# The setup of a fused attention and state-space kernel: zero products on TensorE before x lands, fewer transfers in another order, and six scores ahead of the other chunks' last projections

## The chip, the cores and the metric

The kernel runs on one core of a Trainium2 chip. The metric is the device time of one execution in microseconds (us). Before the change three runs gave 1181.41, 1182.49 and 1183.07: a median of 1182.49.

## The reference

Two independent parts are computed and joined along the last axis. Part A is a diagonal state-space layer: for each of 576 channels a kernel of 2048 taps is summed from 128 complex exponentials, and u is convolved with it. Part B is attention with 32 query heads of width 18 and one shared key and value head, over 2048 positions.

```python
K = jnp.einsum("dn,dnl,dn->dl", Cc, jnp.exp(logdA[:, :, None] * l), dB).real   # part A
a = causal_convolution(u, K) + u * Dskip
q = (x @ wq).reshape(B, S, 32, 18)                                             # part B
k, v = x @ wk, x @ wv
p = softmax(q k^T * 18 ** -0.5);  b = (p v).reshape(B, S, 576) @ wo
return jnp.concatenate([a, b], axis=-1)
```

## The kernel before

**The tiling.** The 2048 positions are four chunks of 512 columns. Part B goes over 1024 score tiles: chunk c of the queries, group g of four heads, block kb of 128 keys, pair j of two heads. A score (`scores`, L492) is two fp16 matmuls of 55 rows: the augmented queries of a pair (`aug`, a ring of five tiles) against the augmented keys (`kaug`). High and low fp16 parts of q and k and one row of offsets stand on those 55 rows, which is why a projection is rounded into a high part (h1, h2) and a low part (l1, l2) and copied by DMA to rows 0, 18 and 36. ScalarE takes the exponential of each score (`exponentials`, L503), into one of ten P tiles. TensorE multiplies P by v (`product`, L793). NS = 3 scores make a round, as three PSUM tiles hold them.

Part A (class `Conv`, L958 on) runs beside it, mostly on VectorE: `arguments` (L1017) and `factors` (L1065) build exponentials, sines and cosines for a slice of 48 channels, `tables`, `kgen` and `back` the rest.

**The setup** (`Attention.setup`, L231) starts both parts. Loads go out on the queues of SP, ScalarE and POOL. `first` (p1) is the projection of x's chunk 0: the first 96 query columns and the keys, in five steps over the model dimension, x0 being loaded in five slices. `rest(k)` (L297) is step k of five for the keys of chunks 1 to 3 (`second`, p2), the last 32 of the first 128 query columns and all values (`vps`); it reads slice k of xr, x's chunks 1 to 3. From `first` come h1 and l1, whose copies fill chunk 0 of `kaug` (`place`, L340) and `aug` 0 and 1 (L318). `km`, `small`, `aw_first` and `bias` bound the scores so that the exponentials cannot overflow. `conv.begin(n)` (L1347) advances part A's first slice by n pieces, which puts these into the order of VectorE and ScalarE at that place. After `rest(4)` come h2 and l2, chunk 1 of `kaug`, and `vt`.

**The order of the work.** The order on TensorE, ScalarE and VectorE is the program's own order; POOL and SP are ordered by the framework. `main` (L740) goes round by round: scores, exponentials, then `fill` puts pieces of the query projections, of the output projection and of part A where a planner's clock (`Clock`, K.t for TensorE, K.v for VectorE, K.a for ScalarE) expects TensorE to wait. After the first round (three scores, r == 0) it calls `settle` (L346), which transposes v, makes `kmax` on TensorE (`kmx`), places chunks 2 and 3 of `kaug`, loads wq 2 to 4 and the rest of part A's inputs, and moves the planner's clock on by 2.0.

Of the kernel before, what the change touches and what calls it, by code (L numbers as in the profile page):

```python
# [17 lines left out]
P = 128  # L18
# [22 lines left out]
FLOOR = LIMIT / (2 * SCALE) * QQ / 60000.0  # L41

NS = 3
NP = 10


# [147 lines left out]
class Attention:  # L194
# [33 lines left out]
    def load_wq(self, m):  # L228
        self.nc.sync.dma_start(self.wq[m], self.a["wq"][m, :, :, :MQ[m][1]])

    def setup(self, tp, conv):  # L231

# [12 lines left out]
        wkv = tp.tile([P, 5, 64], F32, name="wkv_sb")  # L245
        xr = tp.tile([P, 5, 3, CT], F32, name="xr")
# [6 lines left out]
        vt = keys[:, 4, :]  # L253
        self.x0 = x0 = self.xp.tile([P, 5, CT], F32, name="x0", tag="x")

        nc.gpsimd.memset(x0[64:, 4, :], 0.0)
        nc.gpsimd.memset(xr[64:, 4], 0.0)
        for j in range(2):
            nc.gpsimd.memset(self.ring[j], 0.0)
        conv.early()  # L260
        nc.scalar.dma_start(self.wq[0], a["wq"][0])
        nc.sync.dma_start(wkv, a["wkv"])
        for k in range(5):
            n = DT[k][1]
            nc.sync.dma_start(x0[:n, k, :], a["xT"][0, :n, k, :])
        nc.scalar.dma_start(self.sel, a["sel"][:, 0:45])
# [14 lines left out]
        self.o_left = self.q_left = self.units = 0  # L281
        self.todo, self.busy, self.group = [], False, 0
        self.side_work = Stream(self.side(), self.k, 99.0)
        conv.begin(6)
        p1, small = (self.ps_s.tile([P, 2, CT], F32, tag="s", name=n)[:, 0, :] for n in ("first", "small"))
        p2 = self.bank(CT, "second")
        pv = self.ps_o.tile([P, CT], F32, tag="o", name="vps")
# [3 lines left out]
                             start=(k == 0), stop=(k == 4), tile_position=(0, 32 * j))  # L291

        def project(ps, j, i, c, k):
            nc.tensor.matmul(ps[32 * j:32 * j + 32, :], wkv[:, k, i:i + 32], xr[:, k, c - 1, :] if c else x0[:, k, :],
                             start=(k == 0), stop=(k == 4), tile_position=(0, 32 * j))

        def rest(k):  # L297
# [8 lines left out]
            project(p1, 3, 0, 0, k)  # L306
        nc.scalar.activation(h1, p1, AF.Copy, scale=QS)
        self.ab0 = ab = self.p2.tile([P, 2], F32, tag="ab", name="ab0_0")
        V.tensor_reduce(ab[:, 0:1], p1, axis=AX.X, op=ALU.max, apply_absolute_value=True)
        V.scalar_tensor_tensor(l1, p1, QS, h1, op0=ALU.mult, op1=ALU.subtract)  # L310
        V.tensor_scalar(ab[:, 0:1], ab[:, 0:1], QS, None, op0=ALU.mult)
        self.place(0, h1, l1, 96, (nc.sync, nc.sync))
        for pr in range(2):
            for row, src in ((0, h1), (18, h1), (36, l1)):
                for j in range(2):
                    h, b = 2 * pr + j, 64 * j + row
                    q = nc.sync if pr and row == 36 else nc.gpsimd
                    q.dma_start(self.aug[pr][b:b + 18, :], src[h * DH:h * DH + DH, :])  # L318
        V.tensor_scalar(self.km[:, 0:1], ab[:, 0:1], spread[:, 139:140], None, op0=ALU.mult)
# [13 lines left out]
        V.scalar_tensor_tensor(l2, p2, QS, h2, op0=ALU.mult, op1=ALU.subtract)  # L333
        self.place(1, h2, l2, 0, (nc.sync, nc.gpsimd))
        V.tensor_copy(vt, pv)
        V.tensor_reduce(self.km[:, 4:5], p2, axis=AX.X, op=ALU.max, apply_absolute_value=True)
        V.tensor_scalar(self.km[:, 4:5], self.km[:, 4:5], QS, None, op0=ALU.mult)
        self.vt = vt

    def place(self, c, hi, lo, i, qs):  # L340
        for row, t in ((0, hi), (36, hi), (18, lo)):
            for j in range(2):
                b = 64 * j + row
                qs[j].dma_start(self.kaug[b:b + 18, c * CT:(c + 1) * CT], t[i:i + 18, :])

    def settle(self, conv):  # L346

        nc, V, K = self.nc, self.V, self.k
        km, ab, spread = self.km, self.ab0, self.spread
        h2, l2 = self.parts[2:]  # L350
        vp = self.bank(CT, "vp").rearrange("p (j n) -> p j n", j=4)
        for j in range(4):
            nc.tensor.transpose(vp[:, j, :], self.vt[:, j * P:(j + 1) * P], self.ident)
        for src, dst in ((ab[96:, 0:1], ab[96:, 1:2]), (km[96:, 4:5], ab[96:, 0:1]), (ab[96:, 1:2], km[96:, 4:5])):
            V.tensor_copy(dst, src)
        V.tensor_scalar(km[:, 0:4], spread[:, 136:140], km[:, 4:5], None, op0=ALU.mult)
        V.tensor_copy(self.v[:, :, :DH].rearrange("p (c j) d -> p c j d", j=4), vp.rearrange("p j (c d) -> p c j d", c=4)[:, :, :, :DH])
        pk = self.bank(20, "kmx")
        for m in range(5):
            for b, n in ((0, 128),) if m < 4 else ((0, 64), (64, 64)):  # L360
                nc.tensor.matmul(pk[b:b + n, 4 * m:4 * m + 4], spread[:, 2 * m:2 * m + n], km[:, 0:4], start=True, stop=True, tile_position=(0, b))
# [378 lines left out]
    def main(self, conv, flag):  # L740
# [71 lines left out]
        for r in range(0, len(pairs), NS):  # L812
# [145 lines left out]
class Conv:  # L958
# [34 lines left out]
    def load(self, k):  # L993

        if k >= NCK:
            return
        nc = self.nc
        raw = self.p0.tile([P, 6, ND], F32, tag="raw", name=f"raw{k}")
        dt = self.p0.tile([P, ND], F32, tag="dt", name=f"dt{k}")
        nc.sync.dma_start(dt, self.a["ldt"][k * ND:(k + 1) * ND].partition_broadcast(P))  # L1000
        nc.sync.dma_start(raw, self.a["prm"][k])
        self.raw[k] = raw, dt

    def load_u(self, k):
        if k >= NCK:
            return
        nc = self.nc
        ut = self.p0.tile([P, 4, NE], F32, tag="u", name=f"u{k}")
        if k < 2:
            nc.vector.memset(ut[0:1, 0, 0:1], 0.0)  # L1010
        dsk = self.p0.tile([P, NE], F32, tag="dsk", name=f"dsk{k}")
        nc.sync.dma_start(ut, self.a["u"][k])
        nc.sync.dma_start(dsk, self.a["dsk"][k].partition_broadcast(P))
        self.ut[k] = ut, dsk
        self.ut_ready[k % 2] = self.k.t + 10.0

    def arguments(self, k, f, r, m):  # L1017
# [11 lines left out]
        tt(w[:, 0, :], cr, br, op=mu)  # L1029
        tt(w[:, 2, :], ci, bi, op=mu)  # L1030
        tt(w[:, 0, :], w[:, 0, :], w[:, 2, :], op=sb)
        tt(w[:, 1, :], cr, bi, op=mu)
        tt(w[:, 2, :], ci, br, op=mu)
        tt(w[:, 1, :], w[:, 1, :], w[:, 2, :], op=ad)
# [16 lines left out]
        yield "v", 0.0, False  # L1051
        if k == 0:
            tt(m, ch(av, NF), row(1), op=mu)
            yield "v", 0.0, False

    def restore(self, k):
# [342 lines left out]
def build(tc, **aps):  # L1399
# [3 lines left out]
    with ExitStack() as ctx:  # L1403
        clock = Clock()
        at = Attention(tc, ctx, aps, clock)
        cv = Conv(tc, ctx, at.bank, aps, clock)
        cv.at, at.conv = at, cv
        with tc.manual_schedule(engines={mybir.EngineType.PE, mybir.EngineType.Activation, mybir.EngineType.DVE}):
            with tc.tile_pool(name="setup", bufs=1) as tp:
                cv.setup()  # L1410
                at.setup(tp, cv)
            cv.open(ctx)
            at.open(ctx)
            at.main(cv, flag)
    ok = nc.values_load(flag[0:1, 0:1], min_val=0, max_val=1)
    with tc.If(ok < 1):
# [78 lines left out]
```

## Time and profile before

| What | Value |
|---|---|
| median of three runs | 1182.49 us |
| the profiled execution | 1183.13 us, span 1181.4 us |
| TensorE matmul, ScalarE, VectorE, POOL busy | 1090.5, 1032.4, 977.6, 129.6 us |
| mean granted TensorE clock | 0.988 |
| exponentials (L510 and L508) | 992 of 1033 ns, 32 of 1118 ns |
| first matmul, first score, first exponential | 7.86, 26.96, 27.80 us |

The rows in the prediction come from the page and from these views: the timeline of an engine (start, length, engine, line, operation, tiles, count, and in brackets the idle time before and what ended it; neighbours of one kind are merged), the chain of waits in order of time, tables by stretch (length, then busy time of PE, PEld, DVE, ACT and POOL with counts, the granted clock, the DMA share, GB/s), the groups of one tile, and the list of who waited for whom (us in total, times, longest).

### The profile page before, as it was taken

To read this page: it belongs to the slowest core of one execution; us is meant where nothing else is said; L and a number is where in the kernel's file an instruction comes from. 1 tells how busy PE (TensorE), PEld (TensorE's weight loads), DVE (VectorE), ACT (ScalarE), POOL (GpSimd) and SP (SyncE) were. 2 spreads that over 40 slices of the span, in tenths; PEclk is the share of its full clock that TensorE was granted. 3 is DMA by queue.
4 is the path that set the end of the run, shared out by engine and by line. 5 is a ranking of instruction groups with operands and counts; after the bars stand their busy time and mean duration, and the time that the engine had idled before them with its cause. 6 is when DMAs were issued, how large, how long until landed. Compare 5 with 4: busy or idle time off the path is not lost.

```text
span 1181.4 us, 32882 instructions
## 1 busy us (share of the span) xinstructions
PE 1090.5 (92%) x13862; PEld 393.2 (33%) x13862; DVE 977.6 (83%) x1576; ACT 1032.4 (87%) x1090; POOL 129.6 (11%) x233
## 2 busy tenths in 40 slices
PE   6999799999899999899999899999899999989997
PEld 1333233333333333333333333333333333323232
DVE  4678987988988996988998988988978995895923
ACT  3888998888989888998989899898999988898994
POOL 4330301110310100010120200000320000000000
PEclk9899899999999999999999999999999999999999
DMA  7412323122233102033213122012223112011111
GB/s 221 137 52 66 115 88 112 32 57 79 75 124 110 33 28 92 31 104 111 74 50 119 35 86 88 29 57 82 73 67 120 41 38 76 24 56 65 33 42 43
DMA packets 58398, 87.50 MB, mean 74 GB/s; under 512 B 15779, under 2 KB 34839, under 8 KB 57733
## 3 DMA queue, kind: packets, MB, share of 16 engines
q1 hardware_dynamic: 46821, 77.52, 20.5%
q0 software_dynamic: 10848, 7.37, 2.5%
q8 instruction: 110, 1.80, 0.7%
q10 hardware_dynamic: 576, 0.45, 0.1%
q14 instruction: 43, 0.35, 0.1%
HBM read 48.67 MB, written 35.91 MB: 72 GB/s over the span
## 4 chain that ended last, share of the span: by engine, by line
PE 52%; DVE 28%; ACT 10%; issue 6%; DMA 2%; SPq 0%; DVEq 0%; ACTq 0%
PE ops L800 21%; PE s L499 14%; ACT P L510 9%; DVE tab L117 5%; DVE acc L117 5%; PE op L191 4%; DVE ks L117 3%; DVE pt L117 3%; PE iy L191 3%; PE kg L1180 3%; PE q L393 2%; DMA wq_sb<-wq 2%; DVE tt L117 1%; PE hu L191 1%; PE lu L191 1%
## 5 line engine op out<-in xcount | busy, mean ns | idle before, releaser
L510 ACT ACTIVATE P<-s 128x1024 f32<-128x1024 f32 x992 | 935.3, 1033 | 107.0 <-PE s L499 105.4
L800 PE MATMUL ops<-P,v_sb 128*32 128x512 f32 x4096 | 513.5, 599 | 9.6 <-DVE o L121 9.4
L499 PE MATMUL s<-aug,kaug 55*128 55x512 f16 x2048 | 310.0, 383 | 50.1 <-ACT P L510 46.1
L499 PEld LDWEIGHTS <-kaug 55*128 55x128 f16 x2048 | 91.8, 94 | 385.6 <-issue 345.1
L800 PEld LDWEIGHTS ops<-P,v_sb 128*32 128x32 f32 x4096 | 116.8, 110 | 165.2 <-issue 123.8
L443 POOL DMA_DIRECT2D qd<-qh x116 | 66.5, 580 | 475.5 <-DVE qh L125 473.0
L191 PE MATMUL op<-wo_sb,oT 126*32 126x288 f32 (+1 forms) x1152 | 84.0, 416 | 5.5 <-DVE ob L121 2.5
L393 PE MATMUL q<-x,wq_sb 128*32 128x256 f32 x1360 | 85.3, 388 | 1.3 <-DVE un L133 1.3
L117 DVE TENSOR_TENSOR tab<-tab,tt 128x576 f32<-128x576 f32 (+1 forms) x72 | 59.1, 821 | 1.7
L117 DVE TENSOR_TENSOR tab<-r,dif 128x576 f32<-128x576 f32 (+1 forms) x72 | 58.9, 818 | 0.0
L117 DVE TENSOR_TENSOR tt<-f,sum 128x576 f32<-128x576 f32 (+1 forms) x72 | 58.9, 817 | 0.0
L117 DVE TENSOR_TENSOR tab<-sum,r 128x576 f32<-128x576 f32 (+1 forms) x72 | 58.8, 817 | 0.0
L117 DVE TENSOR_TENSOR tab<-tab 128x576 f32<-128x576 f32 (+1 forms) x72 | 58.8, 817 | 0.0
L393 PEld LDWEIGHTS q<-x,wq_sb 128*32 128x32 f32 x1360 | 40.3, 111 | 41.7 <-issue 16.5
L121 DVE COPY ksb<-kg 128x192 f32<-128x192 f32 x48 | 17.5, 364 | 42.9 <-PE kg L1180 42.8
L191 PEld LDWEIGHTS op<-wo_sb,oT 126*32 126x32 f32 (+1 forms) x1152 | 32.7, 111 | 50.0 <-issue 17.1
L117 DVE TENSOR_TENSOR acc<-acc,pt 128x1728 f32<-128x1728 f32 (+2 forms) x36 | 48.6, 1351 | 0.3
L117 DVE TENSOR_TENSOR pt<-us,ks 128x1728 f32<-128x1728 f32 (+2 forms) x36 | 48.3, 1350 | 0.1
L508 ACT ACTIVATE P<-s,bias 128x1024 f32<-128x1024 f32 x32 | 33.1, 1118 | 13.8 <-PE s L499 13.5
L1180 PEld LDWEIGHTS kg<-tab 128*32 128x32 f32 x2304 | 36.2, 110 | 25.8 <-issue 9.5
L1180 PE MATMUL kg<-tab 128*32 128x64 f32 x2304 | 41.7, 220 | 1.9 <-DVE tab L117 1.1
L117 DVE TENSOR_TENSOR ks<-ks 128x576 f32<-128x576 f32 (+1 forms) x48 | 41.0, 854 | 0.6
(155 smaller groups left out, 998.2 us busy)
## 6 DMA issues: line engine op xcount, KB each, us to landing
od<-o SPq DMA_DIRECT2D x31, 256.0 KB
aug<-qd SPq DMA_DIRECT2D x124, 55.0 KB
fr<-stage SPq DMA_DIRECT2D x10, 624.0 KB
u<-u SPq DMA_DIRECT2D x12, 384.0 KB
kd<-ksb SPq DMA_DIRECT2D x12, 384.0 KB
kt<-kd SPq DMA_DIRECT2D x48, 96.0 KB
outa<-u SPq DMA_DIRECT2D x12, 384.0 KB
oT<-od SPq DMA_DIRECT2D x16, 252.0 KB
```

The lines of the kernel that those rows point to most:

```text
L117: return self.v.tensor_tensor(out, *a, **k)
L121: return self.v.tensor_copy(out, *a, **k)
L191: nc.tensor.matmul(ps[j:e], w[:, j:e], x, start=start, stop=stop, tile_position=(0, j))
L393: nc.tensor.matmul(ps[o, 256 * f:256 * f + 256], w[:, k, i], xt[:, k, x], start=(k == 0), stop=(k == 4), tile_position=(0, 32 * j))
L443: q.dma_start(qd[h:h + n, row + d:row + d + nd, cs], src[i1:i1 + n * nd, :cs.stop - cs.start])
L499: nc.tensor.matmul(ps[:, j, :], self.kaug[r, kb * P:(kb + 1) * P], t[r, :], start=True, stop=True)
L508: nc.scalar.activation(pt, ps, AF.Exp, bias=self.bias, scale=SCALE / QQ)
L510: nc.scalar.activation(pt, ps, AF.Exp, scale=SCALE / QQ)
L800: nc.tensor.matmul(o_ps[32 * j:32 * j + 32, :], self.v[:, kb, :], pts[2 * n + j // 2][:, j % 2, :], start=(kb == 0), stop=(kb == 15), tile ...
L1180: nc.tensor.matmul(ps[32 * g:32 * g + 32, d, :], t[:, :32], t[:, 32:], start=(j == 0), stop=(j == 1), tile_position=(0, 32 * g))
```

## The change

Loads. x0 comes in three transfers (slices 0, 1 and 2, 3 and 4) in place of five, all of 128 partitions, so the memsets of the padding go. wq 0 is issued first. sel and spread move from ScalarE's queue to POOL's. xr becomes five tiles, each loaded by one transfer with 6 KB contiguous a partition, on POOL's queue behind a small copy that waits for x0's first slice; they take memory that part A uses later. wq 1 goes out after the copies.

TensorE. Three `matmul4` of zeros (WARM = 3) stand ahead of `first`.

Copies. `aug` 0 and 1 are filled by SP alone, chunk 0 of `kaug` by ScalarE, each set split so that h1's rows go before l1's.

Order. The pieces of part A are begun 4, 2 and 4 instead of 6 and 4, its first slice's coefficients are computed later, and later loads are held by small memsets. `rest(3)` stands behind the first three scores, `rest(4)` and what follows from it (`last`) behind the next three, and `settle` between the eighth and the ninth score. The planner's clock is set to 3.4, 5.3 and at least 8.8 there. POOL's order becomes the program's too.

```diff
+WARM = 3
-        nc.gpsimd.memset(x0[64:, 4, :], 0.0)
-        nc.gpsimd.memset(xr[64:, 4], 0.0)
+        nc.scalar.dma_start(self.wq[0], a["wq"][0])
         conv.early()
-        nc.scalar.dma_start(self.wq[0], a["wq"][0])
+        V.memset(self.wo[:, 0, :], 0.0)
+        warm = self.bank(CT, "warm")
+        for _ in range(WARM):
+            matmul4(nc, warm, self.wo[:, 0, 0:P], self.wo[:, 0, 0:CT])
         nc.sync.dma_start(wkv, a["wkv"])
-        for k in range(5):
-            n = DT[k][1]
-            nc.sync.dma_start(x0[:n, k, :], a["xT"][0, :n, k, :])
-        nc.scalar.dma_start(self.sel, a["sel"][:, 0:45])
-        nc.scalar.dma_start(spread[:, 0:140], a["sel"][:, 45:185])
-        for k in range(5):
-            n = DT[k][1]
-            nc.sync.dma_start(xr[:n, k], a["xT"][1:4, :n, k, :].rearrange("c p n -> p c n"))
+        for k0, k1 in ((0, 1), (1, 3), (3, 5)):
+            nc.sync.dma_start(x0[:, k0:k1, :], a["xT"][0, :, k0:k1, :])
         for b in (54, 118):
             nc.gpsimd.dma_start(self.kaug[b:b + 1, :], a["ones"])
+        nc.gpsimd.dma_start(self.sel, a["sel"][:, 0:45])
+        nc.gpsimd.dma_start(spread[:, 0:140], a["sel"][:, 45:185])
         nc.gpsimd.dma_start(self.ident, a["ident"])
-        self.load_wq(1)
+        nc.gpsimd.tensor_copy(xr[0][0:1, 0, 0:1], x0[0:1, 0, 0:1])
+        for k in range(5):
+            nc.gpsimd.dma_start(xr[k], a["xg"][k * P:(k + 1) * P, CT:].rearrange("p (c n) -> p c n", n=CT))
...
-        conv.begin(6)
+        conv.begin(4)
...
-        self.place(0, h1, l1, 96, (nc.sync, nc.sync))
-        for pr in range(2):
-            for row, src in ((0, h1), (18, h1), (36, l1)):
+        def first(pr, rows, q):
+            for row, src in rows:
                 for j in range(2):
                     h, b = 2 * pr + j, 64 * j + row
-                    q = nc.sync if pr and row == 36 else nc.gpsimd
                     q.dma_start(self.aug[pr][b:b + 18, :], src[h * DH:h * DH + DH, :])
+        self.place(0, h1, l1, 96, (nc.scalar, nc.scalar), (0, 36))
+        first(0, ((0, h1), (18, h1)), nc.sync)
+        self.place(0, h1, l1, 96, (nc.scalar, nc.scalar), (18,))
+        first(0, ((36, l1),), nc.sync)
+        first(1, ((0, h1), (18, h1), (36, l1)), nc.sync)
+        V.memset(self.wq[1][0:1, 0, 0:1], 0.0)
+        self.load_wq(1)
...
-        conv.begin(4)
+        conv.begin(2)
         rest(0)
...
-        for k in range(2, 5):
-            rest(k)
-        V.tensor_scalar(h2, p2, QS, None, op0=ALU.mult)
...
+        conv.begin(4)
+        rest(2)
+        def last():
+            V.tensor_scalar(h2, p2, QS, None, op0=ALU.mult)
+            V.scalar_tensor_tensor(l2, p2, QS, h2, op0=ALU.mult, op1=ALU.subtract)
+            self.place(1, h2, l2, 0, (nc.sync, nc.gpsimd))
+            V.tensor_copy(vt, pv)
...
-        K.t += 2.0
+        K.t = max(K.t, 8.8)
...
+                if i == 8:
+                    self.settle(conv)
                 ss[i] = self.scores(i, c, 2 * g + j, kb, 0.34 if i == r else 0.216)
...
             if r == 0:
-                self.settle(conv)
+                self.rest_of(3)
+                K.t = 3.4
+                continue
+            if r == NS:
+                self.rest_of(4)
+                self.last()
+                K.t = 5.3
+                continue
```

More of the change, by code (lines that the diff above doesn't have):

```diff
@@ L229, in load_wq, with setup @@
         self.nc.sync.dma_start(self.wq[m], self.a["wq"][m, :, :, :MQ[m][1]])
-    def setup(self, tp, conv):
+    def setup(self, conv):
         nc, cp, a, V = self.nc, self.cp, self.a, self.V
@@ L244, in setup @@
         self.kmax = cp.tile([P, 5], F32, name="kmax")
-        wkv = tp.tile([P, 5, 64], F32, name="wkv_sb")
-        xr = tp.tile([P, 5, 3, CT], F32, name="xr")
+        wkv = self.p1.tile([P, 5, 64], F32, tag="db", name="wkv_sb", bufs=2)
+        xr = [(conv.p1 if k < 4 else conv.pf).tile([P, 3, CT], F32, tag=t, name=f"xr{k}") for k, t in enumerate(("us", "ks", "acc", "sc", "tab"))]
         self.km = cp.tile([P, 5], F32, name="km")
@@ L293, in project @@
         def project(ps, j, i, c, k):
-            nc.tensor.matmul(ps[32 * j:32 * j + 32, :], wkv[:, k, i:i + 32], xr[:, k, c - 1, :] if c else x0[:, k, :],
+            nc.tensor.matmul(ps[32 * j:32 * j + 32, :], wkv[:, k, i:i + 32], xr[k][:, c - 1, :] if c else x0[:, k, :],
                              start=(k == 0), stop=(k == 4), tile_position=(0, 32 * j))
@@ L329, in setup, with place @@
         V.tensor_scalar(self.bias, self.bias, -SCALE / QQ, None, op0=ALU.mult)
-        for k in range(2, 5):
-            rest(k)
-        V.tensor_scalar(h2, p2, QS, None, op0=ALU.mult)
[L333 to L341, printed above, removed]
+        conv.begin(4)
[5 more added lines that the diff above has]
+            V.tensor_copy(vt, pv)
+            V.tensor_reduce(self.km[:, 4:5], h2, axis=AX.X, op=ALU.max, apply_absolute_value=True)
+            V.tensor_scalar(self.km[:, 4:5], self.km[:, 4:5], TOP, None, op0=ALU.min)
+        self.vt, self.rest_of, self.last = vt, rest, last
+    def place(self, c, hi, lo, i, qs, rows=(0, 36, 18)):
+        for row in rows:
+            t = lo if row == 18 else hi
             for j in range(2):
@@ L999, in load @@
         dt = self.p0.tile([P, ND], F32, tag="dt", name=f"dt{k}")
+        if k in (1, 2):
+            nc.vector.memset(dt[0:1, 0:1], 0.0)
+            nc.vector.memset(raw[0:1, 0, 0:1], 0.0)
         nc.sync.dma_start(dt, self.a["ldt"][k * ND:(k + 1) * ND].partition_broadcast(P))
@@ L1011, in load_u @@
         dsk = self.p0.tile([P, NE], F32, tag="dsk", name=f"dsk{k}")
+        if k < 2:
+            nc.vector.memset(dsk[0:1, 0:1], 0.0)
         nc.sync.dma_start(ut, self.a["u"][k])
@@ L1028, in arguments, with coefficients @@
         V.tensor_scalar(bv, bv, 1.0 / (2 * math.pi), None, op0=mu)
[L1029 to L1034, printed above, removed]
+        def coefficients():
+            tt(w[:, 0, :], cr, br, op=mu)
+            tt(w[:, 2, :], ci, bi, op=mu)
+            tt(w[:, 0, :], w[:, 0, :], w[:, 2, :], op=sb)
+            tt(w[:, 1, :], cr, bi, op=mu)
+            tt(w[:, 2, :], ci, br, op=mu)
+            tt(w[:, 1, :], w[:, 1, :], w[:, 2, :], op=ad)
+        if k > 0:
+            coefficients()
         yield "v", 0.0, False
@@ L1053, in arguments @@
             tt(m, ch(av, NF), row(1), op=mu)
+            coefficients()
             yield "v", 0.0, False
@@ L1407, in build @@
         cv.at, at.conv = at, cv
[L1408 to L1411, printed above, removed]
+        compute = {mybir.EngineType.PE, mybir.EngineType.Activation, mybir.EngineType.DVE}
+        with tc.manual_schedule(engines=compute | {mybir.EngineType.Pool}):
+            cv.setup()
             cv.open(ctx)
             at.open(ctx)
+            at.setup(cv)
             at.main(cv, flag)
```

4 lines of the change are left out of this document (2 added, 2 removed).

## The prediction

> **What bounds the kernel now.** I read the page first, then the start in time order (engines' timelines, the chain of waits, tables by stretch), because the edits end with the ninth score.
>
> ```profile
> PE 1090.5 (92%) x13862; PEld 393.2 (33%) x13862; DVE 977.6 (83%) x1576; ACT 1032.4 (87%) x1090; POOL 129.6 (11%) x233
> PE s L499 <- ACT P L510: 46.1, 110, 3.2
> 42.90:51.80 8.90, 8.89 (x122) 3.81 (x124) 4.43 (x8) 8.76 (x9) 0.00 (x0) 1.00 0.68 252
> ```
>
> TensorE and ScalarE share the bound. From 42.9 us on neither has room (8.89 and 8.76 busy of 8.90). So what counts is how early this dense part begins: a gain at the start should reach the end nearly whole, if the order of the rest stays as good. The start:
>
> ```profile
> 7.86 1.07 PE L290 MATMUL first<-x,wq_sb 128*32 128x512 f32 x3 [7.86 <-DMA x<-xT]
> 11.24 1.11 PE L290 MATMUL first<-x,wq_sb 128*32 128x512 f32 x3
> 12.10 0.68 PE L290 MATMUL first<-x,wq_sb 128*32 128x512 f32 x3
> 12.59 0.61 PE L290 MATMUL first<-x,wq_sb 128*32 128x512 f32 x3
> 13.88 0.61 PE L290 MATMUL first<-x,wq_sb 128*32 128x512 f32 x3
> 14.56 0.60 ACT L307 ACTIVATE keys<-first 128x512 f16<-128x512 f32 x1 [1.01 <-PE first L294]
> 15.19 7.90 SPq L344 DMA_DIRECT2D kaug<-keys  x6
> 25.13 3.18 DMA aug<-keys
> 28.45 0.59 PE L499 MATMUL s<-aug,kaug 55*128 55x512 f16 x3 [0.24 <-DMA aug<-keys]
> 27.80 3.18 ACT L508 ACTIVATE P<-s,bias 128x1024 f32<-128x1024 f32 x3 [8.36 <-PE s L499]
> 33.13 18.68 ACT L508 ACTIVATE P<-s,bias 128x1024 f32<-128x1024 f32 x18 [2.16 <-PE s L499]
> ```
>
> Nothing runs on TensorE until x lands at 7.86. Its first five rounds of four matmuls are 0.85 us apart, from 12.10 on 0.43. h1 is made at 14.56, its copies go out from 15.19, and the last of them (from the chain: issued at 25.13, 3.18 us under way) lets the second score go at 28.45. Three exponentials run at 27.80; the steady ones start at 33.13, 18 in 18.68 us, 1.038 each, so exponential 9 (counted from 0) begins at 33.13 + 6 x 1.038 = 39.4. That is my yardstick.
>
> **The first projections.** The three zero products are 24 matmuls, six rounds of 0.85 = 5.1 us at the half rate. They need one DVE memset and should lie at about 1.5 to 6.6, where TensorE waits anyway: they cost nothing while x lands after 6.6. If they work, all ten rounds of "first" run at 0.43 and x becomes the limit.
>
> ```profile
> GB/s 2 85 346 351 245 298 377 393 398 260 194 122 60 43 108 143 46 43 171 28 122 206 411 287 300 47 19 77 84 22 86 15 84 146 83 9 131 4 8 0
> 2.13 5.23 SPq L265 DMA_DIRECT2D x<-xT  x5
> SPq L265 <- DMA pos_sb<-pos: 2.6, 1, 2.6
> ```
>
> Here the slices are 2 us. SP's fourth issue on waits for the landing of the transfer eight issues earlier (2.6 us on pos); three x transfers instead of five make eight in all on SP and ACT, so this wait goes and all are out by about 3.5. Then bytes decide: weights, parameters and constants are 0.84 MB by their shapes, x 1.28 MB (the 64 padded rows are loaded now, 0.13 more), together 2.12 MB; 0.17 have moved by 4 us, the rest takes 5.6 us at 350 GB/s, to 9.6. With 1 us to land I take the last slab at 10.6 (9.6 to 11.6). Its two k steps are four rounds, 1.7: "first" ends at 12.3, h1 runs from 12.6 to 13.2. **1.95 us earlier** than before.
>
> **The copies.**
>
> ```profile
> L344 SPq DMA_DIRECT2D kaug<-keys x21: 697/699/927, 15.2 to 39.0; - x21
> L318 POOL DMA_DIRECT2D aug<-keys x10: 505/506/536, 15.8 to 23.8; - x10
> DMA to landing us min/median/max: 3.5/6.8/7.2
> 1.67 0.45 ACTq L266 DMA_DIRECT2D sel_sb<-sel  x1
> SPq L344 <- DMA xr<-xT: 3.2, 1, 3.2
> ```
>
> SP takes 0.70 a copy, 0.74 with its gap. The twelve aug copies now stand on SP alone: issued from 13.25, the sixth at 16.95, the twelfth at 21.4. With the 3.18 above aug 0 lands at 20.1, aug 1 at 24.6 (before: 28.3). The wait on xr (3.2) goes, as xr leaves SP. The six kaug copies stand on ScalarE; no row shows such a copy there, so I bound an issue by its own loads (0.45) and SP's 0.74 and take 0.74, as the shape is SP's: 13.25 to 17.7, ready before aug 1. But they hold up what is behind them on ScalarE.
>
> ```profile
> 5.10 1.28 ACT L1050 ACT_TABLE_LOAD   x1
> 12.31 1.24 ACT L1050 ACTIVATE f<-f 128x1248 f32<-128x1248 f32 x1 [5.93 <-DVE r L125]
> 15.06 1.32 ACT L1098 ACTIVATE r<-r,hp_sb 128x1248 f32<-128x1248 f32 x1
> 16.40 1.28 ACT L1102 ACT_TABLE_LOAD   x1
> 18.19 1.24 ACT L1102 ACTIVATE m<-m 128x1248 f32<-128x1248 f32 x1 [0.51 <-DVE m L117]
> 32.92 0.06 DVE L140 MEMSET wq_sb<- 1x1 f32 x3
> 44.60 0.61 PE L393 MATMUL q<-x,wq_sb 128*32 128x256 f32 x8
> ```
>
> Load, sine, sine, load and exponential are 6.36 us; all but the first load were idle time before the scores. Now the first sine is advanced only after the copies: 17.7 + 6.36 = 24.1 for exponential 0. So the exponentials 0 to 2 run from 24.1 to about 27.3, each as its score is there.
>
> The xr loads, now on POOL, start only once x's first slab is in (about 8): 3.9 MB at some 390 GB/s end near 20 to 21. Slice 2 or 3 is the one that could be late, slices 3 and 4 are needed after 25. sel and spread on POOL cost two issues of 0.51 where POOL is idle and are read after 14. wq 1 goes out at 22 instead of 11 and is first read in the projections after 44. The DVE memsets (0.06 each) only delay loads. The split coefficients and advances of the convolution move the same instructions inside DVE's idle 5.7 us before h2 (its row is below). All of these I put at nothing; without that cover they cost their length, under 2 us together.
>
> **Six scores ahead.**
>
> ```profile
> 22.40 0.63 PE L294 MATMUL second<-xr,wkv_sb 128*32 128x512 f32 x3 [1.54 <-DMA xr<-xT]
> 24.14 0.61 PE L294 MATMUL second<-xr,wkv_sb 128*32 128x512 f32 x3
> 25.25 0.69 DVE L125 TENSOR_SCALAR keys<-second 128x512 f16<-128x512 f32 x1 [5.68 <-PE second L290]
> 28.62 0.23 DVE L125 TENSOR_SCALAR km<-spread_sb,km 128x4 f32<-128x4 f32 x1
> 29.85 0.46 DVE L121 COPY v_sb<-vp 128x288 f32<-128x288 f32 x1 [1.01 <-PE vp L353]
> 30.37 2.18 PE L361 MATMUL kmx<-km,spread_sb 128*128 128x4 f32 x12 [0.55 <-DVE v_sb L121]
> 29.30:36.10 6.80, 6.25 (x31) 2.81 (x31) 3.89 (x13) 4.64 (x5) 4.32 (x9) 0.50 0.32 79
> 25.90:29.30 3.40, 2.11 (x13) 0.74 (x10) 2.76 (x9) 1.50 (x2) 3.10 (x7) 1.00 0.56 72
> 42.86 1.92 PE L800 MATMUL ops<-P,v_sb 128*32 128x512 f32 x16
> 33.88 1.94 PE L800 MATMUL ops<-P,v_sb 128*32 128x512 f32 x8
> ```
>
> A rest step is 24.14 - 22.40 = 1.7; h2 starts 1.1 after the last one began; from h2 to the end of km DVE takes 28.85 - 25.25 = 3.6, then 0.5 for v and 2.2 for kmx. In the changed kernel: scores 1 and 2 at 24.6 to 25.2, rest 3 to 26.9, score 5 when exponential 2 has freed its bank (27.3), rest 4 from 27.6 to 29.3, h2 at 28.7, km 32.3, v 32.8. ScalarE meanwhile does exponentials 3 to 7 until 32.6, which before ended at 38.3. Then kmx, score 8, two products (before three lay ahead of scores 9 to 11) and score 9.
>
> Here the clock decides. From 29.3 to 36.1 it was granted at 0.50, after a stretch with 2.11 us busy in 3.4; kmx took 2.18 and a product 1.94, against 0.96 for one at full clock (1.92 for two). With the full clock: kmx 1.1, score 8 0.3, products 1.7, score 9 and its latency 0.6, exponential 9 at 36.5, 2.9 us gained. At half clock for 3.4 us from 32.7: 38.1, 1.3 gained. At half clock throughout: 40.0, 0.6 lost. TensorE is idle for most of 29.9 to 32.8 in the new order, so a half-clock stretch of some length is to be expected; one of 3.4 us or shorter is nearest to the rows. I take the middle of the first two, **2.1 us**.
>
> [...]
>
> The planner's clock is set to other values after settle, so the order of everything later can differ. Nothing prices that; the nearest row is 46.1 us in 110 waits of the scores on ScalarE, 0.42 each, so four or five waits more or fewer are 2 us either way. I take none.
>
> **Sum.** The steps are read from an execution of 1183.13 us (span 1181.4), 0.6 above the median of 1182.49. 1.95 us from the first projections carry the copies and end, through ScalarE and settle, as about 2.0: 1182.5 - 2.0 = **1180.5** (of the profiled execution, 1181.1), its own range 1179.0 to 1182.0.
>
> **Rivals.**
> 1. *More is gained*: the full clock holds through settle (2.9), or the new order saves waits as well (up to 2 more). For it: ScalarE has eight exponentials done before settle. Against it: the idle 3 us. 1182.5 - 3.9 = 1178.6; chance 0.25.
> 2. *The zeros don't do it*: TensorE falls back to the half rate in the 1.1 us between 6.6 and 7.7, or was never raised. Rounds of 0.85 as before, "first" ends near 14, all later steps move 1.7 back: 1182.2; chance 0.10. Against it: 1.54 us of idle at 22.40 left the clock alone.
> 3. *The new gap lowers the clock*: with 4 us idle before score 1, it falls as it fell after 25.9 to 29.3, and rest 3 runs at half rate, 3.4 instead of 1.7, and rest 4 follows: exponential 9 at 38.3 to 39.9. 1182.5 + 0.1 = 1182.6; chance 0.10.
> 4. *Slower*: aug 1's copies land as late as POOL's did beside the xr loads, 6.8 instead of 3.18 (median row above). Then the twelfth, issued at 21.4, lands at 28.2; as rests 3 and 4 now stand behind score 1, settle moves by 3.6, exponential 9 to 41.7 at the short half clock: 2.3 lost, 1184.8. It decides from 26.7 on, a landing of 5.3. Against it: xr should have ended by 21. Chance 0.13.
>
> [...]
>
> **Chances.** The forecast has 0.42. A measurement of this kernel tells about 0.2% (2.4 us) from no change, so faster means below 1180.1: 0.19 of the forecast and rival 1, 0.44. Within: 0.23 of the forecast and rivals 2 and 3 but for 0.02, 0.41. Slower: rival 4 and that 0.02, 0.15. The range, 1177.0 to 1184.6, leaves out the far end of rival 1 and half of rival 4.
>
> **What would show it.** Right: rounds 0.43 apart from the first x matmul; h1 at 12.6 (no later than 13.5); score 1 near 24.6 and waiting for an aug copy; exponential 0 near 24 behind ScalarE's table loads; exponential 9 at 36.5 to 38. Wrong: x's last slab after 11.6, xr 0 or 2 late on POOL's queue, h2 waiting for more than rest 4, or an end that has moved by another amount than exponential 9, which would be the planner's order.

## The result, and the profile after

Four runs of the changed kernel gave 1199.60 to 1204.61 us, median **1202.49**; four of the kernel before, on the same chip, 1181.41 to 1183.29, median 1182.78. The ratio is 1.0167 (95% interval 1.0143 to 1.0191): **20 us slower**, where 2 us faster was forecast. The profiled execution took 1204.61 us (span 1202.8, mean clock 0.977).

The page's busy times after, then the two waits between TensorE and ScalarE (us in total, times, longest), first after and then the one of before that the prediction did not show:

```profile
PE 1105.6 (92%) x13886; PEld 396.3 (33%) x13886; DVE 979.3 (81%) x1584; ACT 1031.8 (86%) x1090; POOL 129.0 (11%) x229
```
```profile
ACT P L520 <- PE s L509: 122.3, 189, 5.5
PE s L509 <- ACT P L520: 39.2, 96, 2.8
```
```profile
ACT P L510 <- PE s L499: 105.4, 195, 3.0
```

No engine has more work to speak of (TensorE has the 24 matmuls of the three zero products, and its mean granted clock was 0.977, before 0.988). ScalarE waits 17 us longer for scores; TensorE waits 7 less for ScalarE. Now the start, the timelines of TensorE and ScalarE:

```profile
1.57 5.35 PE L192 MATMUL warm<-wo_sb 128*32 128x512 f32 x24 [1.57 <-DVE wo_sb L141]
8.19 0.63 PE L291 MATMUL first<-x,wq_sb 128*32 128x512 f32 x3 [1.27 <-DMA x<-xT]
8.62 0.63 PE L291 MATMUL first<-x,wq_sb 128*32 128x512 f32 x3
10.13 0.79 PE L291 MATMUL first<-x,wq_sb 128*32 128x512 f32 x3 [0.87 <-DMA x<-xT]
10.68 1.09 PE L291 MATMUL first<-x,wq_sb 128*32 128x512 f32 x3
...
14.85 0.61 PE L291 MATMUL first<-x,wq_sb 128*32 128x512 f32 x3
...
28.86 1.76 PE L509 MATMUL s<-aug,kaug 55*128 55x512 f16 x4 [2.98 <-DMA aug<-keys]
...
40.11 1.32 PE L371 MATMUL kmx<-km,spread_sb 128*128 128x4 f32 x12 [1.27 <-DVE v_sb L122]
...
41.90 3.23 PE L810 MATMUL ops<-P,v_sb 128*32 128x512 f32 x16
```
```profile
15.53 0.60 ACT L308 ACTIVATE keys<-first 128x512 f16<-128x512 f32 x1 [9.47 <-PE first L295]
16.16 7.93 ACTq L354 DMA_DIRECT2D kaug<-keys  x6
24.12 1.28 ACT L1078 ACT_TABLE_LOAD   x1 [7.99 <-DMA kaug<-keys]
...
30.34 3.11 ACT L518 ACTIVATE P<-s,bias 128x1024 f32<-128x1024 f32 x3
34.65 5.14 ACT L518 ACTIVATE P<-s,bias 128x1024 f32<-128x1024 f32 x5 [1.20 <-PE s L509]
42.02 1.11 ACT L518 ACTIVATE P<-s,bias 128x1024 f32<-128x1024 f32 x1 [2.22 <-PE s L509]
45.50 12.18 ACT L518 ACTIVATE P<-s,bias 128x1024 f32<-128x1024 f32 x12 [2.37 <-PE s L509]
```

The zeros do what they should: the first two rounds on x are 0.43 apart. Then the second slab is late (0.87 idle), the granted clock falls to 0.50 (10.47 to 13.88), and the rounds are 0.85 apart. h1 is made at 15.53, not at 12.6. Exponential 0 starts at 30.34 (before 27.80), exponential 9 at 45.50 (before 39.4): **6.1 us late**. The other 14 come later. The tables by stretch show how, first before, then after (length, busy time of PE, PEld, DVE, ACT and POOL with counts, clock, DMA share, GB/s):

```profile
350.00:650.00 300.00, 283.64 (x3805) 104.23 (x3798) 264.12 (x429) 270.27 (x289) 22.78 (x40) 1.00 0.24 75
50.00:1150.00 1100.00, 1030.10 (x13320) 372.35 (x13316) 942.52 (x1499) 990.19 (x1047) 110.21 (x193) 0.99 0.22 69
```
```profile
350.00:650.00 300.00, 280.92 (x3712) 102.31 (x3708) 262.33 (x416) 264.27 (x282) 27.82 (x49) 0.99 0.23 73
50.00:1150.00 1100.00, 1024.37 (x13196) 371.45 (x13189) 942.15 (x1494) 976.75 (x1033) 112.40 (x194) 0.98 0.22 71
```

Between 50 and 1150 us ScalarE, which runs the exponentials one behind the other (12 in 12.18 us from 45.50), starts 1033 instructions instead of 1047: 13.4 us of work less in the same time (976.75 instead of 990.19), long after the last edited instruction, and not in one place (from 350 to 650 alone 282 instead of 289). That count is my measure of the loop from here on.

### The profile page after: what moved, and what is told of

It is laid out like the page before. It is cut to its first block, busy times and chain, and to the rows that moved or that the text cites. A ratio compares the mean times of both kernels' runs of the same rounds, so it can differ in the third digit from the quotient of the medians.

```text
span 1202.8 us, 32952 instructions
## 1 busy us (share of the span) xinstructions
PE 1105.6 (92%) x13886; PEld 396.3 (33%) x13886; DVE 979.3 (81%) x1584; ACT 1031.8 (86%) x1090; POOL 129.0 (11%) x229
## 4 chain that ended last, share of the span: by engine, by line
PE 59%; DVE 19%; ACT 13%; issue 6%; DMA 2%; SPq 1%; POOL 0%; ACTq 0%; DVEq 0%
PE ops L810 24%; PE s L509 15%; ACT P L520 12%; PE op L192 5%; DVE tab L118 4%; PE q L403 4%; PE iy L192 3%; PE kg L1209 2%; DVE acc L118 2%; DVE ks L118 2%; PE lk L192 1%; PE lu L192 1%; PE hu L192 1%; DVE stage L118 1%; DVE tt L118 1%
## 5 line engine op out<-in xcount | busy, mean ns | idle before, releaser
L520 ACT ACTIVATE P<-s 128x1024 f32<-128x1024 f32 x992 | 934.7, 1033 | 123.5 <-PE s L509 122.3
L810 PE MATMUL ops<-P,v_sb 128*32 128x512 f32 x4096 | 519.3, 605 | 15.8 <-DVE o L122 15.6
L509 PE MATMUL s<-aug,kaug 55*128 55x512 f16 x2048 | 313.3, 385 | 49.1 <-ACT P L520 39.2
L192 PE MATMUL op<-wo_sb,oT 126*32 126x288 f32 (+1 forms) x1152 | 86.5, 422 | 6.7 <-DVE ob L122 4.6
L489 POOL DMA_DIRECT2D qd<-sh x20 | 14.0, 698 | 262.0 <-DVE sh L126 253.4
```

Source lines behind the costliest of these rows:

```text
L192: nc.tensor.matmul(ps[j:e], w[:, j:e], x, start=start, stop=stop, tile_position=(0, j))
L489: nc.gpsimd.dma_start(qd[h0 + n0:h1, 54, :].rearrange("p (a n) -> p a n", a=2), two(sh, h1 - h0 - n0))
L509: nc.tensor.matmul(ps[:, j, :], self.kaug[r, kb * P:(kb + 1) * P], t[r, :], start=True, stop=True)
L520: nc.scalar.activation(pt, ps, AF.Exp, scale=SCALE / QQ)
L810: nc.tensor.matmul(o_ps[32 * j:32 * j + 32, :], self.v[:, kb, :], pts[2 * n + j // 2][:, j % 2, :], start=(kb == 0), stop=(kb == 15), tile ...
```

## The experiments

**Theory 1**: most of the loss is the order of the main loop, which the planner writes anew because its clocks and counters are other ones after settle; the start costs about 6. **Theory 2**, the rival: the loads, the copies and the memory that they use cost it, and the order is innocent.

**1. The loads without the order.**

```diff
-        rest(2)
...
+        for k in range(2, 5):
+            rest(k)
...
-        K.t = max(K.t, 8.8)
+        K.t += 2.0
...
-                if i == 8:
-                    self.settle(conv)
...
-                self.rest_of(3)
-                K.t = 3.4
-                continue
...
+                self.settle(conv)
```

> The changed kernel with the order put back: rest 3, rest 4 and what follows them stand before the first scores again, settle comes after the first three scores, the planner's clock is moved on by 2.0 as before. Loads, queues, copies and zeros stay as changed. TensorE's order is then that of the kernel before, but for the zeros. Theory 1 (the six scores ahead and the plan that follows from them cost most of it): only the start's loss is left, 1183 to 1189 us. Theory 2 (the loads, the copies and the memory they use cost it, the order is innocent): 1195 us or more.

Measured: 1185.23 against 1183.62, ratio 1.0023 (1.0010 to 1.0037). Exponential 9 stands at 38.8, 0.6 earlier than before, and the count from 50 to 1150 is 1048. This is theory 1's answer. The loads, copies and zeros alone win 0.6 us at the start, and the runs still are 2.7 slower by the ratio (1.6 by the medians); the profiled one (1183.73, near the lowest of its ten) shows no place for that.

**2. The order without the loads.** The other half: before's loads, queues and copies, no zeros, changed order.

> The other half alone: the changed order (six scores ahead, settle before the ninth, the planner's clock as changed), with the loads, queues and copies of the kernel before and no zeros. xr stays in five tiles. TensorE's order is that of the changed kernel but for the zeros. Theory 1: slower than before by 8 to 16 us, 1191 to 1199. Theory 2: within 3 us of the kernel before, 1180 to 1186.

Measured: 1197.90, ratio 1.0127 (1.0104 to 1.0150). The order alone, six scores ahead and plan together, loses 14 us. Its ScalarE timeline and its stretch from 50 us on:

```profile
27.06 3.12 ACT L515 ACTIVATE P<-s,bias 128x1024 f32<-128x1024 f32 x3 [2.82 <-PE s L506]
32.25 5.13 ACT L515 ACTIVATE P<-s,bias 128x1024 f32<-128x1024 f32 x5 [2.07 <-PE s L506]
...
43.49 7.14 ACT L515 ACTIVATE P<-s,bias 128x1024 f32<-128x1024 f32 x7 [2.73 <-PE s L506]
```
```profile
50.00:1150.00 1100.00, 1024.30 (x13222) 371.93 (x13220) 941.68 (x1494) 978.99 (x1036) 112.30 (x194) 0.99 0.22 70
```

Eight exponentials are done by 37.4 (before 38.3), and still the tenth starts at 43.49 instead of 39.4: being ahead was no gain, as settle had moved behind it.

**3. The kernel before with another plan.**

```diff
-        K.v = K.t + 4.0
+        K.v = K.t + 6.3
```

> The kernel before with one number changed: after settle the planner takes VectorE to be 6.3 us ahead of TensorE instead of 4.0. No instruction is added or removed; some 730 of 13862 rows on TensorE change place. If the order alone can move the time by 10 us or more (theory 1): 1185 to 1200. If the time hardly depends on such an order (theory 2): 1179 to 1186.

Measured: 1195.91, ratio 1.0098 (1.0064 to 1.0132). Nothing of the change is in this kernel; one number of the planner costs 12 us (four runs, 1190.72 to 1198.40). Its start is even better than before's (exponential 3 at 32.28 instead of 33.13):

```profile
32.28 18.20 ACT L508 ACTIVATE P<-s,bias 128x1024 f32<-128x1024 f32 x18 [1.15 <-PE s L499]
```
```profile
50.00:1150.00 1100.00, 1018.06 (x13148) 369.32 (x13140) 933.16 (x1484) 977.95 (x1035) 110.35 (x193) 0.98 0.21 68
```

**4. The changed kernel with another plan** (`K.v = K.t + 2.7`).

> The changed kernel with the same number changed: VectorE 2.7 us ahead instead of 4.0. Some 680 rows on TensorE change place, the start is the same up to the ninth score. Theory 1: the time moves by 5 us or more either way, and the difference arises after exponential 12. Theory 2: 1200 to 1205 as the changed kernel.

Measured: 1200.67, ratio 1.0151 (1.0132 to 1.0169), 1.8 below the changed kernel; 1039 instructions. The time did not move by 5. That is theory 2's number and a miss for theory 1 as I had put it; but two plans that differ in 680 rows may be equally poor, so it takes the next experiment to decide. The traces show which plan this is: from exponential 14 on, TensorE, ScalarE and VectorE do the same operations on the same tiles in the same order as in experiment 3. So it is experiment 3's order behind the changed start.

**5. The changed kernel with the plan of before.** The decisive one: start, loads and six scores as changed, but after settle the planner gets the state that it had before.

```diff
+SNAP = {0: (2.892, 6.892, 3.385, [1.635, 2.56, 3.485], 13.14326), 3: ..., 6: ...}
-        K.t = max(K.t, 8.8)
+        K.t = 0.892 + 2.0
...
+            for r in (0, 3, 6) if r == 6 else (r,):
+                if r < 9:
+                    K.t, K.v, K.a, K.s, K.work = SNAP[r]
```

> The changed kernel, start and all, but from the ninth score on the order of the kernel before: after settle the planner's clocks and counters are set to the numbers that they had in the kernel before, so that TensorE, ScalarE and VectorE get the same order as before from about exponential 12 on. Loads, zeros, copies, six scores ahead and the late settle stay. Theory 1 (the plan costs about 14 of the 20 us, the start about 6): exponential 9 at 45 to 46 and 1187 to 1190. Rival (the six scores or the loads upset the main loop whatever its order): 1196 or more.

Measured: **1190.30**, ratio 1.0061 (1.0044 to 1.0078): 12.2 us less than the changed kernel, by the order from the ninth score on alone. Time and exponential 9 (46.27) lie 0.3 above what theory 1 allowed, and far from the rival's 1196.

```profile
42.01 1.12 ACT L518 ACTIVATE P<-s,bias 128x1024 f32<-128x1024 f32 x1 [2.27 <-PE s L509]
46.27 9.40 ACT L518 ACTIVATE P<-s,bias 128x1024 f32<-128x1024 f32 x9 [3.15 <-PE s L509]
```
```profile
350.00:650.00 300.00, 284.33 (x3781) 104.23 (x3777) 263.00 (x425) 270.14 (x289) 26.83 (x48) 0.99 0.24 76
50.00:1150.00 1100.00, 1029.64 (x13322) 372.45 (x13318) 943.01 (x1499) 988.62 (x1046) 110.43 (x193) 0.99 0.23 71
```
```profile
ACT P L520 <- PE s L509: 107.4, 194, 3.3
```

The start is that of the changed kernel (a little worse), the loop that of before: 289 instructions from 350 to 650, 1046 from 50 to 1150, and ScalarE waits 107.4 instead of 122.3. From exponential 14 on, the trace has the three engines' operations in the order of the kernel before. Theory 1 is shown, theory 2 falls.

**6. The order of experiment 2 with the plan of before.**

> The six scores ahead with the loads and copies of the kernel before and no zeros (the second experiment), and from the ninth score on the order of the kernel before. Theory 1: exponential 9 at 43.5 as in the second experiment, 4.1 later than before, and 1185 to 1188. Rival (what six scores ahead cost is not the plan): 1194 or more.

Measured: 1191.89, ratio 1.0074 (1.0057 to 1.0091): 6 us below experiment 2, above the 1185 to 1188 that I expected. Exponential 9 came at 45.9 and not at 43.5. Of these 2.4 us, 1.0 was there at exponential 8 already (40.62 instead of 39.65); the rest is the old plan's three products between scores 8 and 9, which took 5.06 where experiment 2's two took 3.59. The count is 1045.

**7. Six zero products** (experiment 5 with `WARM = 6`).

> The fifth experiment with six zero products in place of three, so that TensorE is busy until x lands. If the drop of the clock before the second slab comes from the idle time ahead of x: the rounds stay 0.43 apart, h1 at 14.4 instead of 15.5, and 1 us less in all. If what follows is set by the small copies beside xr and not by h1: exponential 0 moves by less than 0.5 and the time by less than 0.5.

Measured: 1193.65, ratio 1.0094 (1.0077 to 1.0111). The rounds stay 0.43 apart and h1 comes at 14.05, 1.4 earlier than in experiment 5, and exponential 0 at 29.09, 1.3 earlier. But exponential 9 comes at 46.10 against 46.27: the gain is gone by then. The time is 3 us longer by the medians, though the profiled spans (1190.6 and 1190.8) and counts (1045 and 1046) agree. The profiled execution was the shortest of this kernel's four and the longest of experiment 5's, so the traces can't tell where the 3 us are; that stays open.

**8. kaug's copies off ScalarE** (experiment 5, the six copies issued by POOL).

```diff
-        self.place(0, h1, l1, 96, (nc.scalar, nc.scalar), (0, 36))
+        self.place(0, h1, l1, 96, (nc.gpsimd, nc.gpsimd), (0, 36))
...
-        self.place(0, h1, l1, 96, (nc.scalar, nc.scalar), (18,))
+        self.place(0, h1, l1, 96, (nc.gpsimd, nc.gpsimd), (18,))
```

> The fifth experiment with the first six kaug copies issued by POOL instead of ScalarE. If the sines and the exponential behind those copies on ScalarE set the start: exponential 0 at 25 to 27 instead of 30.3, exponential 9 some 3 us earlier, time 2 to 4 us less. If score 1's copies and the half clock of rest 3, kmx and the products set it: exponential 0 earlier, but exponential 9 within 1 us of the fifth experiment, and so the time.

Measured: 1188.61, ratio 1.0047 (1.0030 to 1.0063). Both theories had a part: exponential 0 comes 3.4 earlier, of which 1.9 are left at exponential 9. The time is 1.7 less, under the 2 to 4 expected, and the two intervals of the ratio (this one and experiment 5's, 1.0044 to 1.0078) overlap.

```profile
26.99 3.12 ACT L518 ACTIVATE P<-s,bias 128x1024 f32<-128x1024 f32 x3 [3.69 <-PE s L509]
...
39.15 1.11 ACT L518 ACTIVATE P<-s,bias 128x1024 f32<-128x1024 f32 x1 [2.98 <-PE s L509]
44.37 11.45 ACT L518 ACTIVATE P<-s,bias 128x1024 f32<-128x1024 f32 x11 [4.10 <-PE s L509]
```
```profile
25.94 1.86 PE L509 MATMUL s<-aug,kaug 55*128 55x512 f16 x6 [5.06 <-DMA aug<-keys]
...
36.50 2.07 PE L371 MATMUL kmx<-km,spread_sb 128*128 128x4 f32 x12 [1.28 <-DVE v_sb L122]
...
39.04 4.96 PE L810 MATMUL ops<-P,v_sb 128*32 128x512 f32 x24
```

TensorE idles 5.06 before score 0 and again during settle, and kmx and the three products run at half rate.

**9. Zeros in those gaps.** Six zero products added into `second` behind rest 2, three in settle.

```diff
         rest(2)
+        for _ in range(6):
+            matmul4(nc, p2, self.wo[:, 0, 0:P], self.wo[:, 0, 0:CT], start=False, stop=False)
...
+        for _ in range(1):
+            matmul4(nc, z0, *zw)
...
+        for _ in range(2):
+            matmul4(nc, z1, *zw)
```

> The eighth experiment (order of before from the ninth score on, kaug's first copies on POOL) with more products of zeros: six, added into second, behind rest 2 where TensorE waits 5.1 us for the copies of aug, one before the transposes of settle and two between them and kmx. If the half clock makes the start of the six-score order late: rest 3 at 0.43 a round, kmx 1.1 instead of 2.07, the three products 2.9 instead of 4.96, exponential 9 at 40.5 to 41.5 instead of 44.4, time 3 to 4 us below the eighth experiment. If it is the chain through rest 4 and settle that costs the time: exponential 9 after 43 and the time within 1.5 us of the eighth experiment.

Measured: **1185.09**, ratio 1.0024 (1.0008 to 1.0039), below experiment 8 by 3.5 (medians) or 2.7 (ratios; the two were run in different sets), as the half clock would have it:

```profile
20.69 5.33 PE L192 MATMUL second<-wo_sb 128*32 128x512 f32 x48
...
36.50 1.27 PE L379 MATMUL kmx<-km,spread_sb 128*128 128x4 f32 x12
...
38.02 2.78 PE L818 MATMUL ops<-P,v_sb 128*32 128x512 f32 x24
```
```profile
26.72 8.14 ACT L526 ACTIVATE P<-s,bias 128x1024 f32<-128x1024 f32 x8 [3.37 <-PE s L517]
38.13 1.12 ACT L526 ACTIVATE P<-s,bias 128x1024 f32<-128x1024 f32 x1 [3.27 <-PE s L517]
41.17 12.45 ACT L526 ACTIVATE P<-s,bias 128x1024 f32<-128x1024 f32 x12 [1.92 <-PE s L517]
```

The products take 2.78 instead of 4.96, kmx 1.27 instead of 2.07, exponential 9 starts at 41.17. The count is 1047. Yet even at the full clock the six-score order starts its dense part 1.8 later than before: exponential 8 waits 3.27 for settle with ScalarE idle.

**10. The order of before with the parts that helped**: experiment 1, kaug's copies on POOL, three zero products in settle.

> The first experiment (loads as changed, order as before: no scores ahead) with kaug's first copies on POOL instead of ScalarE and three products of zeros in settle, one before the transposes and two between them and kmx. The parts of the change that helped, with the order kept. If ScalarE's copies and kmx at half clock were what held the first experiment at an exponential 9 of 38.8: 37 to 38 and a time of 1180.5 to 1182.5. If score 3 stays bound by rest 4 and xr: exponential 9 at 38.5 to 39 and 1182.5 to 1185.

Measured: 1185.70, ratio 1.0028 (1.0017 to 1.0040). Exponential 3 starts at 32.47 (of 33.13 before), exponential 9 at 38.6: by exponential 9 the second answer, score 3 stays bound by what follows rest 4; the time lies just above both ranges. In the profiled execution the loop then loses 4 (count 1043), with the order of before unchanged; the section on idle time and clock below shows what that is. No gain.

**11. A third plan for the kernel before** (`K.v = K.t + 7.0`).

> The kernel before once more with the planner's number changed, VectorE 7.0 us ahead of TensorE after settle instead of 4.0. 587 rows on TensorE change place against before, 679 against the third experiment. If the order of before is one good draw among many: slower than before by 5 us or more, 1188 to 1200. If the third experiment was an unlucky one: 1180 to 1187.

Measured: 1191.51, ratio 1.0070 (1.0055 to 1.0085); 1034 instructions in the profiled run, the slowest of the four (1196.19). Slower by more than 5, the first answer. But it is no further draw: from exponential 14 on, its trace has the order of the changed kernel, as experiment 2's has; experiment 4 has that of experiment 3. So the kernels hold three orders of the loop, each behind the start of before and behind the changed one (ratio to the kernel before):

| Order from exponential 14 on | start of before | changed start, six scores ahead |
|---|---|---|
| of the kernel before | 1 | 1.0061 (experiment 5) |
| of the changed kernel | 1.0070 (experiment 11) | 1.0167 (changed kernel) |
| of experiment 3 | 1.0098 (experiment 3) | 1.0151 (experiment 4) |

In either column the order of before is the fastest. The two others count 1033 to 1039 instructions, the order of before 1043 to 1048 in nine kernels. Three orders are too few to say how good a draw it is.

**12. The kernel before with zeros in its own gaps.**

```diff
+        matmul4(nc, z1, *self.zw)
...
+                if i == 1:
+                    z0 = self.bank(CT, "z0")
+                    for _ in range(2):
+                        matmul4(nc, z0, *self.zw)
```

> The kernel before, its order and loads untouched, with three products of zeros where TensorE waits in its start: two between score 0 and score 1 (it waits there for the copies of aug 1), one between settle's transposes and kmx. If the idle time of 25.9 to 29.3 brought the half clock of 29.3 to 36.1: kmx 1.1 to 1.3 instead of 2.18, score 3 at 31.6 instead of 32.5, exponential 9 at 38.3 to 38.6 instead of 39.4, and 0.8 to 1.1 less time, 1181 to 1182 where before is 1182.3. If the clock falls anyway or score 3 waits for something else: exponential 9 at 39.3 to 40 and no gain.

Measured: 1183.60 against 1182.64, ratio 1.0001 (0.9991 to 1.0010). kmx takes 1.27 instead of 2.18, but the zeros wait until 27.46 (for VectorE's km, by the first row) and push settle back:

```profile
27.46 1.92 PE L191 MATMUL z<-wo_sb 128*32 128x512 f32 x16 [1.33 <-DVE km L133]
...
31.44 1.27 PE L365 MATMUL kmx<-km,spread_sb 128*128 128x4 f32 x12
```

Score 3 starts at 32.64 (before 32.48). What the clock gives, the zeros take. None of the twelve beats the kernel before.

**The sum.** From the changed kernel to before, by the ratios, as the runs were taken in different sets: the order 12.5 us (1.0167 to 1.0061; 12.2 by medians), the copies on ScalarE 1.7 (not clear of the noise), the half clock of the start 2.7 (3.5 by medians), and 2.8 to the kernel before, of which the profile places 1.8 in settle's new place. The other way round, the changed kernel's order costs 8.3 on the start of before (experiment 11) and the changed start 11.5 on top of it. So the order is 8 to 12 of the 20; some 4 us, not much above the noise, arise only where both come together.

**Idle time and clock in the loop.** Between the starts of exponential 12 and of the last one all these kernels do the same matmuls, but for one product (8 matmuls). The traces split what a loop takes longer into TensorE's busy time, which grows when the same matmuls run at a lower clock (in the kernel before a product took 1.94 us at 0.50, 0.96 at the full clock), and its idle time:

| Kernel | us | TensorE busy | idle |
|---|---|---|---|
| before | 1120.4 | 1049.0 | 71.4 |
| changed | 1134.9 | 1057.9 | 77.0 |
| experiment 3 | 1134.9 | 1051.9 | 83.1 |
| experiment 5 | 1122.2 | 1050.2 | 71.9 |
| experiment 10 | 1124.0 | 1052.7 | 71.3 |

Of the 14.5 us that the changed kernel's loop loses, 8.9 are longer matmuls (1.0 of it that product) and 5.6 idle time; it was granted the half clock for 37.5 us, before for 20.5. In experiment 3 it is 2.8 and 11.7. Two orders lose the same by different means. Experiment 10's 3.7 are clock alone, with the order of before: it ran at the half clock at 492.6 for 3.4 us and at 670.1 for 6.8, where before had 3.4 in all.

## Why the prediction was wrong, point by point

- **"The planner's clock is set to other values after settle ... I take none": the step that failed**, by 8 to 12 of the 20 us. I bounded it by 2 us either way from TensorE's waits for ScalarE (46.1 in 110). That is the wrong row: what grows under another order is ScalarE's wait for scores (105.4 before, 122.3 changed, 120.3 in experiment 3), while the 46.1 became 39.2 in the one and 55.7 in the other. And "four or five waits" had no source. No row of before gives a bound; two other orders measured 0.7% and 1.0% on the unchanged start.
- *The zeros* were right to the end of their own work (1.57 to 6.92, rounds of 0.43 on the first slab). "**1.95 us earlier**" failed: h1 came 0.97 later. I let x limit only the last slab; it is the second that left TensorE idle (0.87 us, after 1.27 before the first), and the granted clock fell to 0.50 at 10.47. In experiment 8 the same instructions kept their rounds at 0.43:

```profile
8.11 0.63 PE L291 MATMUL first<-x,wq_sb 128*32 128x512 f32 x3 [1.62 <-DMA x<-xT]
9.97 0.63 PE L291 MATMUL first<-x,wq_sb 128*32 128x512 f32 x3 [0.80 <-DMA x<-xT]
10.43 0.60 PE L291 MATMUL first<-x,wq_sb 128*32 128x512 f32 x3
```

  There h1 came at 13.68, and in experiment 9 at 13.72; in the changed kernel and experiments 4 and 5 at 15.42 to 15.53. So the true size was 0.9 earlier or 1.0 later, by the clock. In experiment 1 the same zeros ended at 5.8, TensorE was idle for 2.40 before x, and the first two rounds on x were 0.82 apart: there rival 2 came true (h1 at 14.41; in experiment 10 at 14.34).
- *The copies.* An issue takes 0.70 as priced, but the twelve stood from 16.20 to 28.37 on SP, 12.17 instead of 8.9. The chain of waits of the changed kernel (start, length, what):

```profile
17.20 5.92 DMA aug<-keys
23.14 0.71 SPq L317
...
27.67 1.89 DMA aug<-keys
```

  The second copy is 5.92 under way beside xr, and SP's sixth copy, at 23.14, goes out only when it has landed (23.12): the wait on the transfer eight issues back on SP and ScalarE together, which I had read from before for x, and did not apply to eighteen copies on two queues. Score 1 went at 28.86, not at 24.6. That is rival 4's lateness (28.2), but through an early copy that stopped the queue and not through the last one, which was 1.89 under way. What stood against this rival, xr in by 20 to 21, was mis-sized: the last of xr's five loads, issued at 11.5, was 12.7 under way, to 24.2 (the tile xr of the changed kernel):

```profile
L275 POOL DMA_DIRECT2D xr<-xg x5: 527/528/623, 9.4 to 11.5; - x5
DMA to landing us min/median/max: 4.8/8.6/12.7
```
- *ScalarE.* Sines and exponential behind the copies, 6.2 us, was right; the copies took 7.93 instead of 4.45 for the same reason, so exponential 0 stood at 30.34 and not at 24.1.
- *Rest 4 and settle behind the scores.* From exponential 0 to 9 I had 12.4 at the full clock, 13.2 with the middle that I took. The changed kernel took 15.2 and experiment 9, at the full clock, 14.5. In between lies one chain (exponential 2, score 5, rest 4, h2 to km on VectorE, kmx, score 8, products, score 9) that before ran beside the copies. Rival 3 came true with it: rest 3 at half rate, the products 3.23. A half-clock stretch of 3.4 us or less was not nearest to the rows: the one shown lasted 6.8 (29.3 to 36.1), and the changed kernel had one of that length, at 27.5, and one of 3.4, at 41.2. I gave each rival a price as if it came alone; here 3 and 4 came together.

```profile
27.50:34.40 6.90, 5.40 (x22) 1.00 (x24) 0.00 (x0) 5.92 (x6) 0.00 (x0) 0.51 0.43 105
41.20:44.60 3.40, 3.40 (x22) 0.83 (x22) 3.09 (x13) 1.11 (x1) 3.40 (x7) 0.50 0.26 58
```

- *Right in part* was that the dense part passes a shift on. With the order of before, exponential 9's delay of 1.8 in experiment 9 is the 1.8 of the span (1183.2 against 1181.4). But in experiments 5 to 8 the span grew by 2.5 to 3.1 more than exponential 9's delay (experiment 5: 9.4 and 6.9), and in experiment 10 by 3.4 after an exponential 9 that was 0.9 early. And the last line named the sign to look for, "an end that has moved by another amount than exponential 9". As a gain it had a price, up to 2 in rival 1; as a loss it had no chance and no price.
- *Small readings.* It is SP's fifth issue, the ninth of SP and ScalarE together, that waits on pos, the first of them. x is 1.31 MB by its shape. The 1 us to land has no row of its own; in experiment 8 the last slab was in by 11.72, where its first round ran without a pause.

## What to carry to other kernels

Where a planner writes the order of the whole kernel from a clock, an edit to that clock is an edit to every instruction behind it; compare the two orders before pricing the start, and give the order a range of its own: here two other orders cost 0.7% to 1.1%. To judge a change of the start in such a kernel, freeze the order behind it (experiment 5), or the draw of the order hides the answer; even then the clock moved the loop by up to 3.7 us (experiment 10). Work put ahead of a serial step gains only if the step itself does not move back by as much.

## What the runs showed of the hardware

- In the kernel before, the rounds on x were 0.85 apart from 7.86 to 12.10 and 0.43 apart from there. In the changed kernel the zeros, 24 matmuls from 1.57, took 5.35 us, and the first two rounds on x were 0.43 apart.
- In the changed kernel TensorE was idle for 1.27 and 0.87 us before the rounds at 8.19 and 10.13, 2.0 us in all between 7.05 and 10.47; then the clock was 0.50 until 13.88, with rounds 0.85 apart. In experiment 5 it was idle for 1.22 and 0.86, and the rounds were 0.85 apart from 10.73 on; in experiment 1 after one pause of 2.40 they were 0.82 apart. In experiment 8, after 1.62 and 0.80, they stayed 0.43 apart, as in experiment 7, where the zeros ran on until x was there. Why they did so in experiment 8, with the longer pause ahead of x, was not shown.
- In the kernel before, TensorE was idle for 1.29 of the 3.40 us from 25.9 to 29.3, and the clock was 0.50 for 6.8 us from there. With 24 zero matmuls in its gaps (experiment 12) kmx took 1.27 us instead of 2.18. With zeros in the gaps of the changed start (experiment 9) kmx took 1.27 and the three products 2.78, where experiment 8 took 2.07 and 4.96.
- In the changed kernel an 18-row copy on SP, issued at 17.20 beside the xr loads (the last of them in at 24.2), was 5.92 us under way; one issued at 27.67 was 1.89. The ten aug copies that POOL issued in the kernel before, from 15.8 to 23.8, had a median of 6.8. The six copies on ScalarE's queue held up ScalarE's own work for 7.93 us.
